# Attention weights turned by a transposing transfer of 16-bit halves, and the last batch's query tiles taken one by one

## The chip, the core and the metric

The kernel runs on one core of a Trainium2 chip. The metric is device time in microseconds from launch to end. The core has TensorE (PE; its weight loads are listed apart as PEld), VectorE (DVE), ScalarE (ACT), GpSimd (POOL) and SyncE (SP), which here only issues transfers (DMAs). Each engine works through its own queue in order; engines wait for each other and for transfers through semaphores.

## What is computed

Top-k attention for 8 batches, 8 heads, 576 rows and head dimension 64, followed by a feed-forward layer on the 4608 x 512 result:

```python
scores = scale * np.matmul(q, k.transpose(0, 1, 3, 2))
kth = np.partition(scores, -top_k, axis=-1)[..., -top_k:-top_k + 1]      # top_k = 32
scores = np.where(scores >= kth, scores, -1000000000.0)
attn = np.exp(scores - np.max(scores, axis=-1, keepdims=True))
attn = attn / (np.sum(attn, axis=-1, keepdims=True) + 1e-09)
x = np.matmul(attn, v)                       # then (B,H,S,D) -> (B*S, H*D)
h = x @ w_in                                 # 512 -> 2048
g = np.where(h > 0.0, h, np.exp(np.minimum(h, 0.0)) - 1.0)
return (g @ w_out).astype(np.float32)        # 2048 -> 512
```

All of it is in 32-bit floats; the two weight matrices come in as 64-bit numbers and are converted at the start.

## The kernel before

**Steps.** The 576 rows of a batch make four query tiles of 128 rows and a rest of 64 (`rem`; the rests of an even batch and the next odd one fill one tile together). One step handles a query tile for two heads (a head pair, `hp`), or the rest for four heads: 128 partitions by two rows of 576 scores, the tile `u.sc`. A batch has 4 x 4 + 2 = 18 steps, the run 144 (`NS`). `orders` says in which order a batch takes its tiles: one by one, `(0,)`, or in pairs, `(0, 1)`, whose steps alternate within a head pair so that one attention product serves both (a `Group`).

**The loop** (lines 809 to 848) runs over n and works on four steps at once, in a pipeline written out by hand:

- step n + 2: `scores`, TensorE (L335) into one pair of PSUM tiles, then ScalarE copies to `u.sc` (L343). Five `sc` buffers.
- step n: `select`, VectorE, in four passes: eight searches for the eight largest (L355, L369) and six replacements (L362). Between the passes the loop issues everything else.
- step n - 1: `spread` (GpSimd L376), `mask` for each of the two rows (ScalarE L396 and L397, with the row's sum), `normalise` (GpSimd L407 to L414).
- step n - 2 (`done`): `turn`, which transposes the weights for the product with v. Nine blocks of 128x128 go through TensorE (L433) into PSUM, and ScalarE copies them to the group's `et` tile (L434), in three calls: four blocks (`main`) and one (`rest`) after the second pass, four (`other`) after the third. Two `et` buffers.
- `attend`, two iterations after a group was turned: TensorE multiplies `et` with `vT` (L459), ScalarE copies into the block's `xT` (L486).

**Feed-forward blocks.** Finished tiles are collected in blocks of one or two tiles (`division`), in the order of `ends`. A block's work comes as pieces: 16 hidden units (`hidden`, L534, then ScalarE L544, L547, L549, L553 and GpSimd L504), and for two tiles seven products by Strassen's scheme (`product`, L624; half of their weights come back from memory in tiles `tw`, prefetched six deep by `stream`, L666), for one tile four projections (`project`, L562). `feed`, called four times in an iteration, is the planner: each block has a due time `ready` in steps (3.25 after its last tile's last step), each piece a cost (`HIDDEN`, `PROJECT`), and `feed` issues as many pieces as keep the due times. What is left after the loop is issued at its end (line 849). Before, there are 21 blocks: five of one tile, fifteen of two, one of one.

**Keys and queries** of the coming batch are loaded a few iterations ahead (L235), and VectorE transposes them in 32x32 blocks (L289) into one of five `kqT` buffers; the previous user of a buffer is an older `scores`.

**Transfers** are all issued from SP's queue, in the order of the program: loads, `tw` prefetches, outputs.

**Start.** `tight` is 2 * NHP = 8 and `settled` 12; the first iterations do some of this in another order while the weights are converted. `settle` opens the pools that take the place of the raw weights.

Of the kernel before, what the change touches and what calls it, by code (L numbers as in the profile page):

```python
# [9 lines left out]
ALU = mybir.AluOpType  # L10
FP32 = mybir.dt.float32
U32 = mybir.dt.uint32
I32 = mybir.dt.int32
PSUM = bass.MemoryType.PSUM

# [65 lines left out]
def kernel(  # L81
# [41 lines left out]
    xpool = pool("x", 2)  # L123
    opool = pool("o", 2)
    scratch = pool("scratch", 1, space=bass.MemoryType.DRAM)
    ps_sc = pool("ps_sc", 1, space=PSUM)
    ps_t = pool("ps_t", 2, space=PSUM)
    ps_f = pool("ps_f", 2, space=PSUM)
# [89 lines left out]
    def decode_piece(i):  # L218
# [153 lines left out]

    def spread(u):

        u.den = small.tile([P, 4], FP32, tag="den", name="den")
        nc.gpsimd.tensor_tensor(  # L376
            u.den[:, 2:4], u.last[:, :, 7], u.first[:, :, 0], ALU.subtract
        )

    def mask(u, i, early=False):  # L380

        if u.masked:
            return
        if i == 0 and early:
            u.den = small.tile([P, 4], FP32, tag="den", name="den")  # L390
# [5 lines left out]
        nc.scalar.activation(sc, sc, AF.Prelu, scale=-1.0, bias=low, alpha=1.0 / STEEP)  # L396
        nc.scalar.activation(  # L397
            sc, sc, AF.Exp, scale=-STEEP, bias=gap, accum_out=u.den[:, i : i + 1]
        )

    def normalise(u):

        if u.normal:
            return
        u.normal = True
        den = small.tile([P, 2], FP32, tag="dene", name="dene")
        nc.gpsimd.tensor_scalar_add(den[:], u.den[:, 0:2], EPS)  # L407
        rec = small.tile([P, 2], FP32, tag="rec", name="rec")
        nc.gpsimd.tensor_tensor(rec[:], den[:], power[:], ALU.pow)
        nc.gpsimd.tensor_tensor(den[:], den[:], rec[:], ALU.mult)  # L410
        nc.gpsimd.tensor_scalar(den[:], den[:], -1.0, 2.0, ALU.mult, ALU.add)
        nc.gpsimd.tensor_tensor(rec[:], rec[:], den[:], ALU.mult)
        for i in range(2):
            nc.gpsimd.tensor_scalar(  # L414
                u.sc[:, i, :], u.sc[:, i, :], rec[:, i : i + 1], 1.0, ALU.mult, ALU.mult
            )

    def turn(u, chunks):

        if u.turned:  # L420
            return
        g = u.group
        if g.et is None:
            g.et = etpool.tile([P, 2 * J + 1, len(g.tiles), P], FP32, tag="et", name="et")
        if chunks.stop - chunks.start == 1:
            ps = wide[1][:, 1, HS : HS + P]
        else:
            ps = ps_t.tile([P, JP], FP32, tag="t", name="eps")
        sc = u.sc[:, :, :].rearrange("p i s -> p (i s)")
        n = chunks.stop - chunks.start  # L430
        for c in range(n):
            c0 = (chunks.start + c) * P
            nc.tensor.transpose(ps[:, c * P : (c + 1) * P], sc[:, c0 : c0 + P], ident[:])  # L433
        nc.scalar.copy(  # L434
            g.et[:, chunks, u.at, :],
            ps[:, 0 : n * P].rearrange("p (c q) -> p c q", c=n),
        )
        if chunks.stop == 2 * J + 1:
            u.turned = True
            if u.at == len(g.tiles) - 1:  # L440
                closing.append((place[0] // 4, g))

    def attend(g):
        t = g.tiles[0]
# [65 lines left out]
    def ffn_pieces(blk):  # L510
# [4 lines left out]
        def hidden(f):  # L515
# [32 lines left out]
            if end % unit == 0:  # L548
                nc.scalar.activation(blk.n, blk.n, AF.Exp, scale=-1.0)  # L549
                dst = g[:, end - unit : end, 0:n_tok]  # L550
                apart = place[0] > 4 * (tight + 3) and blk is not blocks[-1]
                if apart:
                    nc.scalar.activation(blk.n, blk.n, AF.Copy, bias=-1.0)  # L553
                gates.append((place[0], (blk.number, f + 1 - unit), dst, blk.n, apart))
# [254 lines left out]
    for n in range(NS + 3):  # L809
# [30 lines left out]
        next(passes)  # L840
        if prev:
            normalise(prev)
# [42 lines left out]
```

## Time and profile before

| | |
|---|---|
| runs, median of 3 (lowest, highest) | 1583.68 us (1582.25, 1584.01) |
| profiled execution, span from first to last instruction | 1583.3 us |
| instructions | 28148 |
| transfers on SP's queue | 121.38 MB |
| L433 (transposes on TensorE), busy | 175.7 us in 1152, 40.3 us in 144 |
| L434 (their copies on ScalarE), busy | 163.9 us in 288, 38.5 us in 144 |

In the profile, times are in us from the first instruction, unless marked ns. A row of a group gives line, engine, operation, output <- input with shapes and the count, then the busy time and the mean ns of one, then the idle time of the engine just before and what ended it. Rows of a stretch give, after its length, the busy time and count of TensorE, its weight loads, VectorE, ScalarE and GpSimd, then TensorE's granted clock, the transfer engines' busy share and GB/s. Rows of a timeline give start, length, engine, line, operation and count, and idle time with what ended it in brackets; a matmul's length contains its way through the array, so neighbours overlap, and the distance from start to start is what one costs. Waits are given as total us, number, longest.

### The profile page before, as it was taken

The page shows a single profiled execution, that of the slowest core. Times are in us where ns is not written, and L with a number is a line of the kernel's source. Part 1 is how long each engine was busy: PE and PEld are TensorE (multiplying, and loading weights), DVE is VectorE, ACT ScalarE, POOL GpSimd, SP SyncE. Part 2 cuts the span into 40 slices and gives each one's busy share as a digit, 9 for nine tenths or more (in the row PEclk, how much of TensorE's full clock was granted, in tenths as well). Part 3 has the DMA queues.
Part 4 walks back from the last instruction along what each step waited for, and adds up shares of the span by engine and source line. Part 5 has one row for each costly group of instructions (what it writes and reads, how often), then busy time and mean ns, then how long its engine had stood idle before and what let it go on. Part 6 is the DMA issues. An engine that isn't in the chain of part 4 may idle for free.

```text
span 1583.3 us, 28148 instructions
## 1 busy us (share of the span) xinstructions
PE 1522.8 (96%) x9492; PEld 1189.1 (75%) x9492; DVE 1450.6 (92%) x2976; ACT 1189.6 (75%) x2460; POOL 901.2 (57%) x1551
## 2 busy tenths in 40 slices
PE   4789989999999999999999999999999999999999
PEld 2477667767777778877887788877777777887786
DVE  6899999999999999999999799999999789999600
ACT  6897678768696968696878787868777777878642
POOL 4983455555656565656565647564646555656550
PEclk9879999999999999999999999999999999999999
DMA  8622202231504141334223412314140514030311
GB/s 244 191 81 37 38 28 57 55 88 39 154 4 136 31 124 28 96 69 110 57 81 71 108 50 79 96 54 105 34 125 9 142 27 132 9 120 1 120 53 34
DMA packets 224910, 123.46 MB, mean 78 GB/s; under 512 B 182272, under 2 KB 183296, under 8 KB 224768
## 3 DMA queue, kind: packets, MB, share of 16 engines
q1 hardware_dynamic: 223568, 121.38, 28.6%
q8 instruction: 75, 1.23, 0.3%
q14 instruction: 67, 0.55, 0.1%
q10 hardware_dynamic: 1200, 0.30, 0.1%
HBM read 108.00 MB, written 13.63 MB: 77 GB/s over the span
## 4 chain that ended last, share of the span: by engine, by line
PE 71%; DVE 17%; ACT 5%; issue 3%; POOL 3%; DMA 0%; SPq 0%; DVEq 0%; POOLq 0%; ACTq 0%
PE hps L534 25%; PE ops L624 23%; PE avps L459 9%; PE scps L335 9%; DVE wk L362 8%; DVE m L369 6%; PE eps L433 5%; DVE m L355 2%; ACT sc L397 1%; POOL sc L414 1%; DVE raw L192 1%; PE scps L433 1%; ACT et L434 1%; POOL gT L504 1%; ACT sc L396 0%
## 5 line engine op out<-in xcount | busy, mean ns | idle before, releaser
L369 DVE MAX8 m<-wk 128x8 f32<-128x576 f32 x864 | 609.6, 747 | 0.0
L534 PE MATMUL hps<-xT,w_in 128*128 128x256 f32 (+1 forms) x2688 | 550.0, 354 | 0.0
L534 PEld LDWEIGHTS hps<-xT,w_in 128*128 128x128 f32 x2688 | 444.3, 192 | 64.1 <-issue 22.7
L362 DVE MATCH_REPLACE8 wk<-m,wk 128x576 f32<-128x576 f32 x576 | 423.5, 743 | 0.0
L407 POOL TENSOR_SCALAR dene<-den 128x2 f32<-128x2 f32 x144 | 32.3, 225 | 411.4 <-ACT sc L397 410.2
L397 ACT ACTIVATE sc<-sc,den 128x576 f32<-128x576 f32 x288 | 223.5, 776 | 52.6 <-POOL den L376 40.0
L335 PE MATMUL scps<-kqT 64*128 64x288 f32 (+1 forms) x1280 | 211.5, 447 | 37.4 <-ACT et L434 23.3
L396 ACT ACTIVATE sc<-sc,m 128x576 f32<-128x576 f32 x288 | 224.9, 781 | 28.7 <-DVE m L369 28.7
L414 POOL TENSOR_SCALAR sc<-sc,rec 128x576 f32<-128x576 f32 x288 | 213.5, 751 | 14.9
L624 PE MATMUL ops<-tw,gT 128*128 128x256 f32 x960 | 219.8, 382 | 1.9 <-issue 1.9
L355 DVE MAX8 m<-sc 128x8 f32<-128x576 f32 x288 | 202.0, 743 | 11.8 <-ACT sc L343 11.8
L362 DVE MATCH_REPLACE8 wk<-m,sc 128x576 f32<-128x576 f32 x288 | 211.6, 743 | 0.0
L624 PEld LDWEIGHTS ops<-tw,gT 128*128 128x128 f32 x960 | 177.8, 190 | 32.6 <-issue 6.5
L343 ACT ACTIVATE sc<-scps 128x576 f32<-128x576 f32 x288 | 170.8, 646 | 37.4 <-PE scps L335 37.3
L459 PE MATMUL avps<-et,vT 128*64 128x256 f32 (+2 forms) x2320 | 191.9, 314 | 2.9 <-ACT et L434 2.9
L504 POOL TENSOR_TENSOR gT<-n,gT 128x512 f32<-128x512 f32 x136 | 173.5, 1276 | 35.9 <-ACT n L553 35.9
L335 PEld LDWEIGHTS scps<-kqT 64*128 64x128 f32 (+1 forms) x1280 | 112.5, 183 | 105.1 <-ACT et L434 33.5
L459 PEld LDWEIGHTS avps<-et,vT 128*64 128x64 f32 x2320 | 130.0, 142 | 72.8 <-issue 36.0
L433 PE MATMUL eps<-ident,sc 128*128 128x128 f32 x1152 | 175.7, 277 | 2.1 <-POOL sc L414 1.6
L433 PEld LDWEIGHTS eps<-ident,sc 128*128 128x128 f32 x1152 | 143.4, 143 | 34.2 <-issue 7.0
L434 ACT COPY et<-eps 128x512 f32<-128x512 f32 x288 | 163.9, 569 | 6.3 <-PE eps L433 5.8
L624 PE MATMUL ops<-w_out,gT 128*128 128x256 f32 x720 | 165.4, 383 | 0.0
(56 smaller groups left out, 1534.3 us busy)
## 6 DMA issues: line engine op xcount, KB each, us to landing
tw<-kept SPq DMA_DIRECT2D x240, 256.0 KB, 3.0
raw<-in_moe_w_in_dram SPq DMA_DIRECT2D x16, 512.0 KB, 4.9
vT<-in_v_dram SPq DMA_DIRECT2D x64, 128.0 KB, 2.5
raw<-in_moe_w_out_dram SPq DMA_DIRECT2D x16, 512.0 KB, 4.4
out_dram<-osb SPq DMA_DIRECT2D x32, 256.0 KB, 3.7
kin<-in_k_dram SPq DMA_DIRECT2D x112, 72.0 KB, 2.8
qin<-in_q_dram SPq DMA_DIRECT2D x112, 72.0 KB, 2.6
kept<-tw SPq DMA_DIRECT2D x16, 256.0 KB, 2.1
```

The source lines that it names most:

```text
L335: nc.tensor.matmul(wide[i][rows, half, 0:HS], kq[part, q0 : q0 + u.t.ql], kq[part, k0 : k0 + HS], start=True, stop=True,)
L355: nc.vector.max(found[i], cur[i])
L362: nc.vector.match_replace(wk[i], found[i], cur[i], TAKEN)
L369: nc.vector.max(found[i], cur[i])
L396: nc.scalar.activation(sc, sc, AF.Prelu, scale=-1.0, bias=low, alpha=1.0 / STEEP)
L397: nc.scalar.activation(sc, sc, AF.Exp, scale=-STEEP, bias=gap, accum_out=u.den[:, i : i + 1])
L414: nc.gpsimd.tensor_scalar(u.sc[:, i, :], u.sc[:, i, :], rec[:, i : i + 1], 1.0, ALU.mult, ALU.mult)
L433: nc.tensor.transpose(ps[:, c * P : (c + 1) * P], sc[:, c0 : c0 + P], ident[:])
L459: nc.tensor.matmul(ps[i * D : (i + 1) * D, cols], vt[:, 2 * J + i if c == J else i * J + c, :], w, start=(c == 0), stop=(c == J),)
L504: nc.gpsimd.tensor_tensor(dst, n, dst, ALU.add)
L534: nc.tensor.matmul(blk.h[:, f % bank, :], w_in[:, i, f * P : (f + 1) * P], blk.xT[:, i, 0:n_tok], start=(i == 0), stop=(i == NC - 1),)
L624: nc.tensor.matmul(sums, x[:, f, :], w, start=opens and f == 0, stop=f == NG - 1, skip_group_check=not opens,)
```

## The change

1. *Turning.* In iterations n > `settled`, `turn` is replaced. `split(done, 0)`, before the first pass, and `split(done, 1)`, after the second, each copy one row's 576 words on ScalarE into a tile of two planes of 16-bit halves (`planes`, one buffer, low halves then high halves) and write it from SP to a tile in device memory (`halves`, three buffers). `cross(done)`, after the third pass, reads that tile back with one transposing transfer of 16-bit elements, 256 rows (query, half) by 1152 columns (row of scores, key), into the group's `et` tile: 9 blocks of 128 partitions by 256 halves, which are 128 words. Nothing of the weights' value is changed.
2. *Last batch.* Its query tiles are taken one by one, as the first batch's are, and the last five tiles make five blocks of one tile. There are then 23 blocks: five of one tile, thirteen of two, five of one.
3. *Small things.* The denominator's helper columns live in one tile of eight columns; the condition under which a block's gates are closed on GpSimd is now `blk.ready < NS` instead of `blk is not blocks[-1]`.

```diff
+    halves = pool("halves", 3, space=bass.MemoryType.DRAM)
...
+        late["p"] = ctx.enter_context(tc.tile_pool(name="p", bufs=1))
...
-        den = small.tile([P, 2], FP32, tag="dene", name="dene")
-        nc.gpsimd.tensor_scalar_add(den[:], u.den[:, 0:2], EPS)
-        rec = small.tile([P, 2], FP32, tag="rec", name="rec")
+        den, rec = u.den[:, 4:6], u.den[:, 6:8]
+        nc.gpsimd.tensor_scalar_add(den, u.den[:, 0:2], EPS)
...
+    def split(u, i):
+
+        if u.turned:
+            return
+        if i == 0:
+            u.halves = halves.tile([P, 2, 2, S], U16, tag="h", name="halves")
+        t = late["p"].tile([P, 2, S], U16, tag="p", name="planes")
+        words = u.sc[:, i, :].bitcast(U16).rearrange("p (k w) -> p w k", w=2)
+        nc.scalar.copy(t[:], words)
+        nc.sync.dma_start(u.halves[:, :, i, :], t[:])
+
+    def cross(u):
+
+        if u.turned:
+            return
+        g = u.group
+        if g.et is None:
+            g.et = etpool.tile([P, 2 * J + 1, len(g.tiles), P], FP32, tag="et", name="et")
+        nc.sync.dma_start_transpose(
+            g.et[:, :, u.at, :].bitcast(U16),
+            u.halves[:].rearrange("q w i k -> (q w) (i k)"),
+        )
+        turned(u)
+
+    def turned(u):
+
+        u.turned = True
+        if u.at == len(u.group.tiles) - 1:
+            closing.append((place[0] // 4, u.group))
...
-                apart = place[0] > 4 * (tight + 3) and blk is not blocks[-1]
+                apart = place[0] > 4 * (tight + 3) and blk.ready < NS
...
-        if b == 0:
+        if b in (0, B - 1):
             order = [(0,), (1,), (2,), (3,)]
...
-        n = 1 if len(blocks) <= J else 2
+        n = 1 if len(blocks) <= J or len(ends) <= J + 1 else 2
...
+        crossed = n > settled
+        if done and crossed:
+            split(done, 0)
         next(passes)
         feed(n, 0.25)
...
-        if done:
+        if done and not crossed:
             turn(done, main)
             turn(done, rest)
+        elif done:
+            split(done, 1)
         if prev:
             mask(prev, 1, n <= tight)
         next(passes)
         feed(n, 0.25)
-        if done:
+        if done and not crossed:
             turn(done, other)
+        elif done:
+            cross(done)
```

More of the change, by code (lines that the diff above doesn't have):

```diff
@@ L12 @@
 U32 = mybir.dt.uint32
+U16 = mybir.dt.uint16
 I32 = mybir.dt.int32
@@ L373, in spread @@
     def spread(u):
-        u.den = small.tile([P, 4], FP32, tag="den", name="den")
+        u.den = small.tile([P, 8], FP32, tag="den", name="den")
         nc.gpsimd.tensor_tensor(
@@ L389, in mask @@
         if i == 0 and early:
-            u.den = small.tile([P, 4], FP32, tag="den", name="den")
+            u.den = small.tile([P, 8], FP32, tag="den", name="den")
         u.masked = i == 1
@@ L405, in normalise @@
         u.normal = True
-        den = small.tile([P, 2], FP32, tag="dene", name="dene")
-        nc.gpsimd.tensor_scalar_add(den[:], u.den[:, 0:2], EPS)
-        rec = small.tile([P, 2], FP32, tag="rec", name="rec")
[L409 to L412, printed above, removed]
+        den, rec = u.den[:, 4:6], u.den[:, 6:8]
+        nc.gpsimd.tensor_scalar_add(den, u.den[:, 0:2], EPS)
+        nc.gpsimd.tensor_tensor(rec, den, power[:], ALU.pow)
+        nc.gpsimd.tensor_tensor(den, den, rec, ALU.mult)
+        nc.gpsimd.tensor_scalar(den, den, -1.0, 2.0, ALU.mult, ALU.add)
+        nc.gpsimd.tensor_tensor(rec, rec, den, ALU.mult)
         for i in range(2):
@@ L438, in turn @@
         if chunks.stop == 2 * J + 1:
-            u.turned = True
-            if u.at == len(g.tiles) - 1:
-                closing.append((place[0] // 4, g))
+            turned(u)
[18 more added lines that the diff above has]
+        )
+        turned(u)
+    def turned(u):
+        u.turned = True
+        if u.at == len(u.group.tiles) - 1:
+            closing.append((place[0] // 4, u.group))
     def attend(g):
```

## The prediction

> **What bounds the kernel now.** I read the busy table, then the busy times by stretch, then who waited for whom, and last the order of time around the end.
>
> ```profile
> PE 1522.8 (96%) x9492; PEld 1189.1 (75%) x9492; DVE 1450.6 (92%) x2976; ACT 1189.6 (75%) x2460; POOL 901.2 (57%) x1551
> ```
> ```profile
> 0.00:80.00 80.00, 46.45 (x193) 30.53 (x194) 63.13 (x126) 61.05 (x123) 53.36 (x84) 0.91 0.71 215
> 80.00:800.00 720.00, 706.62 (x4563) 542.91 (x4563) 720.00 (x1479) 563.20 (x1164) 413.46 (x738) 0.98 0.27 68
> 800.00:1300.00 500.00, 493.17 (x2998) 391.70 (x2997) 475.33 (x977) 383.68 (x796) 289.89 (x500) 1.00 0.30 77
> 1300.00:1480.00 180.00, 177.34 (x1176) 143.25 (x1175) 180.00 (x374) 139.10 (x291) 110.02 (x189) 1.00 0.24 72
> 1480.00:1584.00 104.00, 99.19 (x568) 80.67 (x568) 12.13 (x24) 42.53 (x88) 34.43 (x44) 1.00 0.19 59
> ```
> ```profile
> DVE kqT L289 <- PE scps L335: 24.7, 2, 16.6
> ```
> ```profile
> 1487.95 1.41 DVE L369 MAX8 m<-wk 128x8 f32<-128x576 f32 x2
> ```
> ```profile
> 1484.69 3.62 PE L624 MATMUL ops<-tw,gT 128*128 128x256 f32 x16
> 1488.24 2.38 PE L459 MATMUL avps<-et,vT 128*64 128x256 f32 x20
> ...
> 1519.43 1.31 PE L459 MATMUL avps<-et,vT 128*64 128x128 f32 x20
> 1520.67 3.72 PE L534 MATMUL hps<-xT,w_in 128*128 128x256 f32 x16
> ...
> 1551.57 14.45 PE L534 MATMUL hps<-xT,w_in 128*128 128x128 f32 x128
> 1565.87 13.90 PE L562 MATMUL ops<-w_out,gT 128*128 128x512 f32 x32
> ```
> ```profile
> 1579.85 0.58 ACT L571 COPY osb<-ops 128x512 f32<-128x512 f32 x1 [12.18 <-issue]
> 1580.46 0.33 SPq L574 DMA_DIRECT2D out_dram<-osb  x1
> ```
>
> Two engines are full at once. VectorE's top-k search ends at 1489.4 us (1487.95 + 1.41), and up to there it stood still for only 41.5 us: 16.9 in the first 80 us (80 − 63.13), and 24.7 between 800 and 1300, where the key and query transposes of L289 waited for TensorE's scores. TensorE is the one that is late: when VectorE has finished, TensorE is only at the attention product of 1488.24, where iteration 143 begins, so it lags by one iteration, and has 91.5 us of work left (to 1579.8). Copy and store add 3.5 us to the span of 1583.3. So the span is 1447.8 us of VectorE work before the search ends (1450.6 less 2.8 of gates in the tail), 41.5 of stalls, and a tail of 93.9.
>
> **The change, part by part.** *Turning, from iteration 13 on.* The condition is `n > settled`, with `settled` = 8 + 4, so the steps 11 to 143 change, 133 of 144. (The change's few words say 21; I count by the code.) Off TensorE go nine transposes a step, off ScalarE three copies:
>
> ```profile
> 700.35 0.60 PE L433 MATMUL eps<-ident,sc 128*128 128x128 f32 x4
> 700.79 0.27 PE L433 MATMUL scps<-ident,sc 128*128 128x128 f32 x1
> 700.90 1.89 PE L534 MATMUL hps<-xT,w_in 128*128 128x256 f32 x8
> 702.63 0.60 PE L433 MATMUL eps<-ident,sc 128*128 128x128 f32 x4
> 703.06 1.89 PE L534 MATMUL hps<-xT,w_in 128*128 128x256 f32 x8
> ```
> ```profile
> 702.88 0.57 ACT L434 COPY et<-eps 128x512 f32<-128x512 f32 x1
> 703.34 0.27 ACT L434 COPY et<-scps 128x128 f32<-128x128 f32 x1
> 703.50 0.78 ACT L396 ACTIVATE sc<-sc,m 128x576 f32<-128x576 f32 x1
> ...
> 705.09 0.57 ACT L544 ACTIVATE n<-hps 128x512 f32<-128x512 f32 x1
> ...
> 707.24 0.57 ACT L434 COPY et<-eps 128x512 f32<-128x512 f32 x1
> 707.70 1.19 ACT L343 ACTIVATE sc<-scps 128x576 f32<-128x576 f32 x2
> ```
>
> Start to start, since neighbours overlap, that is 0.44 + 0.11 + 0.43 = 0.98 us of TensorE and 0.62 + 0.46 = 1.08 us of ScalarE a step: 130 and 144 us in all.
>
> ScalarE gets two copies of 1152 half-words (`split`), a form that the trace lacks:
>
> ```profile
> L396 ACT ACTIVATE sc<-sc,m 128x576 f32<-128x576 f32 x288 | 224.9, 781 | 28.7 <-DVE m L369 28.7
> L553 ACT ACTIVATE n<-n 128x512 f32<-128x512 f32 x136 | 85.8, 631 | 4.3
> L184 ACT ACTIVATE w_in<-raw 128x512 int32<-128x512 uint32 x16 | 10.6, 663 | 0.0
> ```
>
> The two L434 copies give 0.30 us for 384 more elements (0.46 less 0.16), 0.78 ns each, so 1152 from L553's 0.63 come to 1.13 us, and 1.04 start to start. That is the low end; the high end is L396 twice over, 1.56. L184 reads every second word and costs 5% more than L553, so I stay near the low end: 1.04. ScalarE then has 1189.6 − 144 + 277 = 1323 us, below VectorE's need. Behind a `split` on ScalarE's queue stand the next mask and the FFN's activations, and for those TensorE's banks wait. The first copy of a step waits for GpSimd's normalising of the iteration before:
>
> ```profile
> 1495.44 0.23 POOL L407 TENSOR_SCALAR dene<-den 128x2 f32<-128x2 f32 x1 [5.85 <-ACT sc L397]
> ...
> 1497.39 1.48 POOL L414 TENSOR_SCALAR sc<-sc,rec 128x576 f32<-128x576 f32 x2
> ```
>
> Its first half is ready 2.7 us after the mask (1495.44 to 1497.39, and half of 1.48); the score copies and FFN activations in between cover that. The second waits until the first write has left the one `planes` buffer; a mask (1.6 us), two feeds and mostly the wait for VectorE lie between. In an iteration with two groups of FFN hidden units ScalarE has two masks of 1.6 (703.50 to 705.09), two `split`s, score copies of 1.2 and two groups of 2.15 (705.09 to 707.24), 10.8 us against VectorE's 10.1 (1447.8 / 144), so over the four such iterations of a block it falls back some 3 us, and recovers in the products. The scores are two iterations ahead and absorb this, except where L289 needs the newest scores; for that I add 3 us.
>
> SP's queue gets three transfers a step:
>
> ```profile
> q1 hardware_dynamic: 223568, 121.38, 28.6%
> ```
> ```profile
> DMA packets 224910, 123.46 MB, mean 78 GB/s; under 512 B 182272, under 2 KB 183296, under 8 KB 224768
> ```
> ```profile
> tw<-kept SPq DMA_DIRECT2D x240, 256.0 KB, 3.0
> kin<-in_k_dram SPq DMA_DIRECT2D x112, 72.0 KB, 2.8
> kept<-tw SPq DMA_DIRECT2D x16, 256.0 KB, 2.1
> ```
>
> Two writes of 288 KB in runs of 1152 B land like `kept<-tw`, in 2.1 to 2.4 us. The transposing transfer of 576 KB is unknown. Its bounds: q1's mean rate, 121.38 MB in 28.6% of the span or 268 GB/s, gives 2.2 us of all sixteen engines; cut into 128-byte packets (72 KB key loads consist of these), 4608 at q1's mean of 32 ns give 9.3 us. Its source rows lie in one piece of 2304 B, nearest to the 2 KB rows of `tw`, so I take 2.2, landing in about 4. A step of 10.1 us has 7.2 us free of the present 28.6%, and the writes take 2.2, so 5 are left. In front of the reader lies more than an iteration: `cross` comes in the third quarter of n, `attend` at n + 2.
>
> `cross` makes SP wait for the second write, 2 to 3 us, and behind it on SP stand the `tw` prefetches (six tiles ahead, 0.9 us of TensorE each), key and query loads (four iterations early), value loads and outputs. A prefetch that is late by 3 us sometimes stops TensorE; it has the room shown below. If that room were gone, it is the third rival.
>
> *The last batch.* Query tiles one by one and five blocks of one tile replace two blocks of two (tiles 7,4 with 7,0 and 7,1 with 7,2). A single block takes 28.2 us (1551.57 to 1579.8). A block of two takes 16 hidden units of 1.73 (700.90 to 702.63) and seven products of 3.55 (1484.69 to 1488.24), 52.5. So two times 3.9 more, and four attention products of 1.25 twice instead of 2.31 once, 0.8: TensorE pays 8.6 us. What counts is what may start only at the end: before, a block of two and a single one; now two singles.
>
> *No time:* the denominator's columns in one tile (the same five GpSimd operations), and `blk.ready < NS` (only the last block, at 147.25, is out, as before).
>
> **The sum.** TensorE: 1522.8 − 130 + 8.6 = 1401 us. Of that 60 come after the search, so 1341 plus 33.6 idle in the first 80 us must fit before it: 90 us or 0.7 a step to spare. Then the 24.7 us of L289 vanish, and the search ends at 1489.4 − 24.7 + 3 = 1467.7. By the planner's own due times, worked through for the new blocks, TensorE has at the start of iteration 144 still 14 hidden units of 0.90 and the four projections (13.9) of the block of tile 7,2, four attention products of 1.25, and the last block, 28.2: 59.7 us. The last weights need, after the search, two masks and a `split` between (4.5), GpSimd (2.7 to the first half), `split`, write, `split`, write (6.8) and the transfer (4 to 5): 18 to 19 us, and TensorE gets to them after 20. With 3.5 for copy and store the tail is 63.2. The sum is 1467.7 + 63.2 = **1531 us**, 52 below the span of this execution, which is the runs' median within 0.4 us.
>
> **Rivals.** *The transposing transfer is slow.* Were it cut as fine as the key loads, 9.3 us, a step would need 2.9 + 2.2 + 9.3 = 14.4 us of the transfer engines against 10.1: 133 × 4.3 = 570 us more, some 2100 us. It decides from about 5.4 us on, where 133 steps lose the 52 us. For it: no transfer of this kind is in the trace. Against: long source rows, rings three quarters idle. The Trainium skill, "VectorE: DVE Perf Modes", The three transpose paths, gives 1309 ns for one 128x128 of 16 bits by transfer, against 390 on TensorE; 18 such one after another would be an estimated 23.6 us a step, and some 3300 us in all. "DMA: Bandwidth & Descriptors", Latency and other measured facts, gives 261 GB/s for whole transposing transfers, about q1's rate here. No run so far shows which holds.
>
> *ScalarE becomes the bound.* With 1.56 us a copy it has 1189.6 − 144 + 415 = 1461 us, all of the time to the end of the search, and it also waits in order; at 97% use the search ends near 1506 and the time is about 1570. For it: 75% busy, growing most where it is fullest. Against: L184 and L553.
>
> *SP holds up TensorE.* Thirteen blocks of two with two late prefetches of 3 to 4 us each give 80 to 100 us, the whole room; the stalls of L289 return and the time is near 1560 to 1585.
>
> *Only the tail is won*, because L289 still waits for other reasons: 1531 + 22 = 1553.
>
> **How the numbers follow.** Forecast 0.60 (own range 1516 to 1548: TensorE one iteration ahead or behind its place at the end, 9 us, and a late last transfer). Only the tail 0.08. ScalarE 0.10 (0.07 faster, 0.01 same, 0.02 slower). SP 0.07 (0.04, 0.02, 0.01). Slow transfer 0.15, all slower. About 0.2% is what a measurement of this kernel tells from no change. Faster 0.79, same 0.03, slower 0.18. The range runs from 1516 to 1592: it leaves out the slow transfer and some 0.05 beside it.
>
> **What would show it.** Right: TensorE's L433 rows are left with 11 steps, its busy time is near 1400; the `split` rows read near 1.1 us; the transposing transfer's median to landing is under 6 us; L289 waits for nothing; VectorE's search ends near 1468 and TensorE's tail is two blocks of 28 us. Wrong: VectorE waiting for score copies over many steps with the transfer share near 1 (slow transfer), ScalarE over 97% busy, or SP's waits passed on to L624.

## The result and the profile after

| | before | after |
|---|---|---|
| median (lowest, highest) | 1582.97 us (1582.16, 1584.01), 4 runs | 1837.77 us (1836.1, 1838.11), 4 runs |
| span of the profiled execution | 1583.3 us | 1835.6 us |
| predicted | | 1531 (1516 to 1592) |

The ratio is 1.1608, with a 95% interval of 1.1592 to 1.1624. The kernel became 255 us slower where 52 us less were forecast.

The busy table of the kernel after, engine by engine:

```profile
PE 1496.8 (82%) x8535; PEld 1109.2 (60%) x8535; DVE 1460.6 (80%) x2976; ACT 1316.5 (72%) x2321; POOL 875.2 (48%) x1535
```

No engine is full any more. VectorE has the same work as before (1460.6 against 1450.6) and now stands still for a fifth of the span. The stretch in the middle of the run, with the columns of the view of before:

```profile
200.00:1700.00 1500.00, 1218.51 (x6852) 914.86 (x6853) 1234.87 (x2526) 1086.99 (x1885) 718.89 (x1272) 0.92 0.61 156
```

There VectorE works 82% of the time, TensorE 81%, ScalarE 72%, the transfer engines 61%: a loop of waits, not a full engine. The view of waits names them (us in total, times, longest):

```profile
ACT planes L451 <- DMA halves<-planes: 245.1, 93, 8.0
DVE m L358 <- ACT sc L346: 221.0, 79, 11.9
...
PE ops L654 <- DMA tw<-kept: 79.2, 20, 10.8
...
DVE kqT L292 <- PE scps L338: 51.7, 3, 24.3
...
PE avps L489 <- DMA et<-halves: 48.9, 29, 4.0
```

The reader follows it backwards. VectorE waits for ScalarE's copies of the scores (221.0) and at the key transposes for TensorE's scores (51.7); ScalarE waits 245.1 us at its half-word copies, nearly all of it at the second one of a step, for the write of the first, because there is one `planes` buffer; and TensorE has a wait that it did not have before, for the prefetched tiles `tw`. The two VectorE waits together, 272.7 us, are nearly the whole of the 276.5 us by which the search ends later than forecast: at 1742.76 + 1.41 = 1744.2 instead of 1467.7 (11.8 us of them stand at the start of the kernel before too).

```profile
1742.76 1.41 DVE L372 MAX8 m<-wk 128x8 f32<-128x576 f32 x2
```

What the queues do shows in the waits of SP, first of the kernel before, then of the one after:

```profile
SPq L666 <- PE ops L624: 686.5, 222, 52.5
```
```profile
SPq L452 <- ACT planes L451: 452.4, 157, 6.8
SPq L461 <- DMA halves<-planes: 242.2, 110, 5.4
...
SPq L696 <- PE ops L654: 18.8, 33, 1.3
```

Before, SP stood at the next `tw` prefetch and waited for TensorE to free a tile: whenever TensorE took one, the next load left at once. After, SP stands at ScalarE's copies and at the writes, and reaches the prefetch when the tile has long been free (18.8 us of waiting in place of 686.5). With each `tw` load paired in the trace with the product that freed its tile, the load left 0.03 us (median) after that before the change, and 5.1 us after it; 143 of the 208 were over 3 us late. At TensorE's 20 waits for `tw` the loads were 7.2 us late on average and took 3.1 us to land, where the median before was 3.0: what stops TensorE is the late issue and not a slow transfer. The new issues in the view of one tile (nanoseconds least/median/most of SP's own time, then first and last start, then a column that is empty here):

```profile
L452 SPq DMA_DIRECT2D halves<-planes x266: 533/553/1033, 171.6 to 1785.1; - x133
L461 SPq DMA_TRANSPOSE et<-halves x133: 2115/2536/4354, 178.2 to 1787.7; - x133
```

133 steps between 171.6 and 1785.1 are some 12.2 us a step (the last two lie behind the end of the search), against 10.1 forecast. One step in the order of time (start, length, engine; the idle time and what ended it in brackets):

```profile
845.31 5.42 PE L654 MATMUL ops<-tw,gT 128*128 128x256 f32 x24
...
847.99 1.15 ACT L451 COPY planes<-sc 128x1152 uint16<-128x1152 uint16 x1 [1.43 <-POOL sc L416]
848.59 2.15 SPq L238 DMA_DIRECT2D kin<-in_k_dram  x4
...
850.84 2.07 SPq L238 DMA_DIRECT2D qin<-in_q_dram  x4
...
853.01 0.55 SPq L452 DMA_DIRECT2D halves<-planes  x1
...
853.66 2.03 SPq L696 DMA_DIRECT2D tw<-kept  x4
...
855.76 1.15 ACT L451 COPY planes<-sc 128x1152 uint16<-128x1152 uint16 x1 [4.72 <-DMA halves<-planes]
...
856.60 3.78 PE L654 MATMUL ops<-tw,gT 128*128 128x256 f32 x8 [5.87 <-DMA tw<-kept]
...
860.31 1.32 PE L338 MATMUL scps<-kqT 64*128 64x288 f32 x8
...
862.35 1.42 DVE L358 MAX8 m<-sc 128x8 f32<-128x576 f32 x2 [3.58 <-ACT sc L346]
```

The first copy is done at 849.14, but its write leaves only at 853.01: SP is issuing eight key and query loads, which the program places ahead of it. So ScalarE stands 4.72 us before the second copy; the `tw` loads, which come behind the write in the program, leave at 853.66, three microseconds after TensorE has used up its tiles (845.31 + 5.42 = 850.7), and TensorE stands 5.87 us; the next scores come behind that product, at 860.31, and VectorE waits 3.58 us for them. Summed over the trace's rows, the first write of a step starts 1.8 us after its copy's end on average, 238 us in all: 124 us of it directly behind query loads (26 times), 75 behind value loads (22) and 22 behind a transposing transfer (19). ScalarE's other work covers some 3.1 us between the two copies: where the first write left within 0.3 us (55 steps), the second copies waited 22 us in all; where it left over 3 us late (40 steps), 177.

### The profile page after: what moved, and what is told of

It reads as the page before. It is cut to its first block, busy times and chain, and to the rows that moved or that the text cites. A ratio compares the mean times of both kernels' runs of the same rounds, so it can differ in the third digit from the quotient of the medians.

```text
span 1835.6 us, 26765 instructions
## 1 busy us (share of the span) xinstructions
PE 1496.8 (82%) x8535; PEld 1109.2 (60%) x8535; DVE 1460.6 (80%) x2976; ACT 1316.5 (72%) x2321; POOL 875.2 (48%) x1535
## 4 chain that ended last, share of the span: by engine, by line
ACT 26%; PE 22%; DMA 18%; DVE 11%; POOL 10%; SPq 7%; issue 6%; DVEq 0%; ACTq 0%; POOLq 0%
DMA halves<-planes 14%; ACT planes L451 8%; PE ops L654 8%; PE hps L564 5%; DVE wk L365 5%; ACT sc L399 4%; ACT sc L400 4%; PE ops L592 4%; DVE m L372 3%; PE avps L489 3%; DMA tw<-kept 3%; POOL sc L416 2%; SPq L238 2%; PE scps L338 2%; ACT sc L346 2%
## 5 line engine op out<-in xcount | busy, mean ns | idle before, releaser
L564 PE MATMUL hps<-xT,w_in 128*128 128x256 f32 (+1 forms) x2944 | 574.1, 354 | 96.1 <-ACT gT L577 91.7
L564 PEld LDWEIGHTS hps<-xT,w_in 128*128 128x128 f32 x2944 | 487.6, 203 | 179.2 <-ACT gT L577 104.0
L451 ACT COPY planes<-sc 128x1152 uint16<-128x1152 uint16 x266 | 306.8, 1153 | 308.7 <-DMA halves<-planes 245.1
L358 DVE MAX8 m<-sc 128x8 f32<-128x576 f32 x288 | 203.3, 747 | 222.4 <-ACT sc L346 221.0
L410 POOL TENSOR_SCALAR den<-den 128x2 f32<-128x2 f32 x144 | 32.3, 225 | 719.6 <-ACT sc L400 718.5
L654 PEld LDWEIGHTS ops<-tw,gT 128*128 128x128 f32 x832 | 167.1, 207 | 141.2 <-DMA tw<-kept 89.1
L489 PE MATMUL avps<-et,vT 128*64 128x128 f32 (+2 forms) x2400 | 199.3, 316 | 53.5 <-DMA et<-halves 48.9
L416 POOL TENSOR_SCALAR sc<-sc,den 128x576 f32<-128x576 f32 x288 | 213.5, 751 | 14.9
L489 PEld LDWEIGHTS avps<-et,vT 128*64 128x64 f32 x2400 | 138.8, 145 | 124.6 <-issue 52.9
L654 PEld LDWEIGHTS ops<-w_out,gT 128*128 128x128 f32 x624 | 125.5, 207 | 78.8 <-POOL den L410 26.7
L592 PE MATMUL ops<-w_out,gT 128*128 128x512 f32 x320 | 145.1, 606 | 0.7 <-POOL tw L711 0.7
```

The costliest lines, as they stand in the source:

```text
L416: nc.gpsimd.tensor_scalar(u.sc[:, i, :], u.sc[:, i, :], rec[:, i : i + 1], 1.0, ALU.mult, ALU.mult)
L451: nc.scalar.copy(t[:], words)
L489: nc.tensor.matmul(ps[i * D : (i + 1) * D, cols], vt[:, 2 * J + i if c == J else i * J + c, :], w, start=(c == 0), stop=(c == J),)
L564: nc.tensor.matmul(blk.h[:, f % bank, :], w_in[:, i, f * P : (f + 1) * P], blk.xT[:, i, 0:n_tok], start=(i == 0), stop=(i == NC - 1),)
L592: nc.tensor.matmul(blk.o[:], blk.gT[f // NG][:, f % NG, s * P : (s + 1) * P], w_out[:, f, :], start=(f == 0), stop=(f == NF - 1),)
L654: nc.tensor.matmul(sums, x[:, f, :], w, start=opens and f == 0, stop=f == NG - 1, skip_group_check=not opens,)
```

## The experiments

Every kernel below differs from the one after, or from an earlier experiment where that is said, by the diff shown; the diffs give the lines that matter, with `...` where some between them are left out. A time without a number of runs beside it is a single run; runs of the kernel before, taken beside them, lie between 1582 and 1586 us.

**Which of the two parts loses.** `e1_last_only` keeps only the last batch's order and single blocks; `e2_turn_only` keeps only the turning.

```diff
-        crossed = n > settled
+        crossed = False
```
```diff
-        if b in (0, B - 1):
+        if b == 0:
...
-        n = 1 if len(blocks) <= J or len(ends) <= J + 1 else 2
+        n = 1 if len(blocks) <= J else 2
```

> The last batch one by one and five last blocks of one tile, every step turned on TensorE as before. If the loss lies wholly in the new way of turning, this is not slower than before: TensorE pays 8.6 us more, the tail falls from 93.9 to about 70, so 1560 to 1575. If the single blocks are themselves a loss (TensorE was full), 1585 or more.

> The transposing transfer alone, last batch as before. If the loss lies wholly in the turning, 1837 plus the 10 to 25 us that the last batch's order wins: 1845 to 1865, with ScalarE waiting some 245 us for the planes buffer as in the changed kernel. If the two parts hurt each other, below 1800.

e1: 1587.3 us (1586.29 to 1587.65, 10 runs), ratio 1.0023 (1.0013 to 1.0032). e2: 1854.4. The loss is wholly in the turning; the last batch's part is worth 17 us beside it, and by itself costs 3. The last search of e1 says why:

```profile
1497.56 1.41 DVE L372 MAX8 m<-wk 128x8 f32<-128x576 f32 x2
```

TensorE is as full as before, with 3 us more work (1526.0 against 1522.8), and the shorter tail (1585.4 less 1499.0, 86.4 us against 93.9) is paid by a search that ends 9.6 us later (1499.0 against 1489.4).

**The loads ahead of the first write.** `e3_loads_after` issues the iteration's loads behind the first copy and write.

```diff
     for n in range(NS + 3):
-        for fn, args in todo.pop(n, []):
-            fn(*args)
...
             split(done, 0)
+        for fn, args in todo.pop(n, []):
+            fn(*args)
```

> Only the order on SP's queue is changed: an iteration's key, query and value loads are issued behind the first write of the planes, not ahead of it. Theory of the order: in the changed kernel the first write starts on average 1.8 us after its copy has ended, 238 us in all, nearly all of it behind these loads; ScalarE's wait for the planes falls from 245 us to 100 to 150, and the time to 1700 to 1760. Rival, ScalarE's work is too much: the time stays above 1810. Rival, the transfer engines are too full (their share 0.63): writes still take 2.8 us and more, the time stays above 1810.

1735.0 us, 103 less. The waits:

```profile
DVE m L358 <- ACT sc L346: 124.1, 50, 11.8
ACT planes L451 <- DMA halves<-planes: 121.9, 78, 5.4
...
PE ops L654 <- DMA tw<-kept: 74.3, 23, 10.5
```

ScalarE's wait for the first write is halved and VectorE's falls by 97, nearly the whole gain; the wait for `tw` stays. First writes still leave 81 us late in all, 58 of it directly behind the transposing transfer of the step before.

**The second copy later.** `e4_split_late` puts the second copy behind the second mask, in the third quarter, and the transposing transfer at the end of the iteration.

```diff
-        elif done:
-            split(done, 1)
         if prev:
             mask(prev, 1, n <= tight)
...
         elif done:
-            cross(done)
+            split(done, 1)
...
         feed(n, 0.25)
+        if done and crossed and late_cross:
+            cross(done)
```

> The second copy of a step comes a quarter later, behind the second mask, and the transposing transfer at the end of the iteration; loads still ahead of the first write. Theory of the one planes buffer: between the two copies there are now two masks, 3.3 us, and FFN work, more than the 2.7 us of a write that starts in time, so ScalarE's wait for the planes falls to 60 to 120 us (what the loads hold up beyond 5 us stays) and the time to 1650 to 1720. Rival, SP is held up by the wait in front of the transposing transfer and its 2.7 us of issue: prefetches of tw are as late as before, the time stays above 1780.

1862.6 us, slower, against my expectation.

```profile
ACT planes L451 <- DMA halves<-planes: 304.5, 160, 7.1
```

The wait grew from 245.1 to 304.5 and from 93 times to 160: with two writes an iteration through one buffer, a copy moved away from one write stands before the next. Here the next step's first copies wait 130 us for the second write, and the second copies still 175 for the first. Moving the copy does not cure it. The run moves the transposing transfer too, and TensorE's wait for `et` grows from 48.9 to 151.1 us; the two moves were not timed apart here.

**No wait for the buffer.** When the second copy begins, row 0 of the score tile is dead. `e5_dead_row` writes the second planes there; `e6_dead_loads` adds e3's order.

```diff
-        t = late["p"].tile([P, 2, S], U16, tag="p", name="planes")
+        if i == 0:
+            t = late["p"].tile([P, 2, S], U16, tag="p", name="planes")[:]
+        else:
+            t = u.sc[:, 0, :].bitcast(U16).rearrange("p (w k) -> p w k", w=2)
```

> The second copy of a step writes its planes over the first row of the score tile, which is dead by then, so that no copy waits for the write of the other; loads are ahead of the first write as in the changed kernel. Theory of the one buffer: ScalarE's wait for planes falls from 245 us to under 40, the time to 1640 to 1720. Rival, the moved loads are the cause and the buffer only passes their delay on: as the write is still late, the transposing transfer and the attention product are late instead, the time stays above 1760.

> Dead row, and the loads behind the first write. Theory of the one buffer: without it the order of the loads matters little, so within 25 us of the kernel with the dead row alone. Rival, order and buffer add: 60 us or more below it. In both, TensorE's wait for tw of some 75 us stays, since the wait ahead of the transposing transfer stays on SP.

1711.4 and 1717.6 us. With the wait for `planes` gone, the order of the loads is worth nothing (6 us the wrong way): the 103 us of e3 and the 126 of e5 are largely the same loss, met at two places. But the wait has moved, and VectorE still waits behind it, here in e5:

```profile
ACT sc L346 <- DMA halves<-sc: 121.4, 60, 6.7
...
DVE m L358 <- ACT sc L346: 95.3, 47, 11.7
```

The score tile is now held until the second write has read it.

**The transposing transfer later.** `e7_cross_late` is e3 with `cross` at the iteration's end (as in e4); `e8_all_three` is e6 with it.

> One planes buffer, loads behind the first write (1735 us so far), and the transposing transfer issued at the end of the iteration, behind the last quarter's prefetches. If SP's wait for the second write (245 us) makes prefetches late, TensorE's wait for tw falls from 74 us to under 40 and the time to 1690 to 1715. If ScalarE's chain sets the pace, the time stays within 15 us of 1735, and the attention products wait more for et.

> Dead row, loads behind the first write, transposing transfer at the end of the iteration. If these three waits are the whole of the loss, the sum of the prediction holds again: 1531 to 1570. If something else is left (ScalarE's work in order, transfer engines), 1600 or more.

1780.0 (45 more than e3) and 1726.5 (9 more than e6), both outside what was expected of a cure. In e7 TensorE waits 102.8 us for `et`, in e3 67.0:

```profile
PE avps L488 <- DMA et<-halves: 102.8, 33, 8.3
...
PE ops L653 <- DMA tw<-kept: 66.6, 18, 9.4
```

The wait for `tw` only falls from 74.3 to 66.6 (second row): moving `cross` does not free the `tw` loads, and later it is itself too late.

**Another queue for the prefetch.** `e9_tw_act` is e3 with the `tw` loads issued from ScalarE.

```diff
-        nc.sync.dma_start(t[:], src[:].rearrange("p (f n) -> p f n", f=TF))
+        nc.scalar.dma_start(t[:], src[:].rearrange("p (f n) -> p f n", f=TF))
```

> Loads behind the first write (1735 us), and the prefetches of tw issued from ScalarE's queue in place of SP's. Theory of the shared queue: SP now stands at ScalarE's copies and at the transposing transfer, so a prefetch that TensorE has made room for is issued up to an iteration late; from another queue TensorE's wait for tw falls from 74 us to under 20, and the time to 1650 to 1690. Rival, the transfers themselves are slow beside the new traffic (tw lands in 3.8 us against 3.0): the wait stays above 50 us and the time above 1715.

1779.1 us, slower than e3 by 44.

```profile
ACT planes L451 <- DMA halves<-planes: 175.8, 75, 6.3
...
PE ops L654 <- DMA tw<-kept: 41.8, 19, 6.9
```

TensorE's wait fell by 32, but ScalarE, which now also issues, waits 54 us more. ScalarE is where SP stood: a load still leaves 4.1 us (median) after its tile is free, as in e3, so that changing the queue leaves the prefetch tied to the same place in the program.

**A second planes buffer, and its control.** `e10_planes2` is e3 with two `planes` buffers; the room comes from five `tw` tiles instead of six and a smaller pool. `e18_control` has the same room taken away, but one `planes` buffer.

```diff
-    TF, TB = 2, 6
+    TF, TB = 2, 5
...
-        late["p"] = ctx.enter_context(tc.tile_pool(name="p", bufs=1))
+        late["p"] = ctx.enter_context(tc.tile_pool(name="p", bufs=2))
```

> Loads behind the first write, and two planes buffers (paid for by five tw tiles in place of six and fewer small buffers). Neither copy waits for the other's write, nor does a score tile wait for one. If the one buffer is the main loss: ScalarE's wait for planes under 15 us, time 1620 to 1680. If SP's queue is the main loss, the wait goes and the time stays above 1690, with TensorE's wait for tw at 75 us or more.

> Loads behind the first write, one planes buffer, and the five tw tiles and fewer small buffers of the kernel with two. If these two are harmless, 1725 to 1745 (1735 without them), and the second buffer is worth some 40 us; if five tiles make prefetches later, 1760 or more, and the second buffer is worth that much more.

1693.3 and 1750.2 us: the second buffer is worth 57, the room taken from the prefetch and the small pool costs 15 (e18 against e3). ScalarE's wait for the write is down to 3.3 us in e10; TensorE's for the prefetch is no smaller, as the second of the two cases expected:

```profile
PE ops L655 <- DMA tw<-kept: 81.0, 22, 10.8
...
DVE m L359 <- POOL den L380: 62.1, 35, 4.4
...
DVE kqT L293 <- PE scps L339: 48.3, 3, 20.4
```

VectorE hardly waits for score copies any more (16.6 us), but for GpSimd to read the results of earlier steps, of which the smaller pool holds fewer, and at the key transposes as in the kernel after.

**More queues.** `e11_tw_act_planes2` is e10 with e9's edit; `e12_and_loads_pool` moves the key and query loads to GpSimd as well (`nc.gpsimd.dma_start` at L238).

> Both: two planes buffers and the prefetches on ScalarE's queue. If buffer and queue are the two causes: 1550 to 1610, TensorE's wait for tw under 20 us. If ScalarE's own work sets the pace by now (1316 us and the issues of the prefetches), 1620 to 1660, with ScalarE over 85% busy and no wait of its own above 50 us.

> As the last one, and key and query loads issued from GpSimd's queue: SP has only writes, transposing transfers, values and outputs. If SP's 4.4 us of issue for a head pair's loads still delays writes: 10 to 40 us below the last one. If GpSimd's normalising is held up by the issues instead: not faster, with ScalarE's wait for L416 above 60 us.

1698.5 and 1698.1 us: no gain, and e11 lies above both of its forecasts. In e11 TensorE's wait moved from `tw` (81.0 to 31.4 us) to `et` (66.9 to 99.3):

```profile
PE avps L490 <- DMA et<-halves: 99.3, 31, 8.9
```

In e12 ScalarE's wait for GpSimd's L417 grew from 46.7 to 85.7 us, the second of its two cases.

**How much is the prefetch?** `e13_no_prefetch` is e10 without the `tw` loads after the first five: the products read those five tiles again, so a part of the weights in them is not the right one.

```diff
-                        t = streamed.pop(0)
+                        t = streamed[taken[0]]
+                        taken[0] += 1
...
+        if k >= TB:
+            streamed.append(streamed[-TB])
+            return
```

> Two planes buffers, loads behind the first write (1693 us), and the prefetches of tw left out after the first five: the products read the same five tiles over and over, so that part of the weights is wrong. Theory of the tied prefetch: TensorE's 81 us of waiting for tw go and with them ScalarE's and GpSimd's waits for products; 1600 to 1640. Rival, ScalarE's work sets the pace: above 1665.

1578.8 us, 114 less than e10, less than either case allowed, and level with before. Its busy table and VectorE's waits:

```profile
PE 1414.1 (90%) x8535; PEld 1063.5 (67%) x8535; DVE 1451.9 (92%) x2976; ACT 1307.6 (83%) x2321; POOL 878.9 (56%) x1535
```
```profile
DVE kqT L293 <- PE scps L339: 12.5, 2, 12.2
...
DVE m L359 <- POOL den L380: 9.0, 8, 2.3
```

Of e10's two waits of VectorE, 110.4 us, 21.5 are left: they hung on the prefetch. The run removes the tiles' lateness, their issue and their bytes together, and does not say which of the three it is. That e11 made the loads less late (1.7 us at the median, e10 3.3) without a gain speaks against lateness alone.

**How much is ScalarE's work?** `e14_half_copy` is e10 with half of each row copied; the planes are two fixed tiles, zeroed once, so that the second half of the keys is zero in them and left out of the attention product. `e16_pool_split` is e10 with the copies on GpSimd.

```diff
-        nc.scalar.copy(t[:], words)
+        nc.scalar.copy(t[:, :, 0:HS], words[:, :, 0:HS])
```
```diff
-        nc.scalar.copy(t[:], words)
+        nc.gpsimd.tensor_copy(t[:], words)
```

> Two planes buffers, loads behind the first write, and only the first half of each plane copied (576 of 1152 elements), the other half left at zero; all transfers as before. It takes 0.48 us from each of 266 copies, 128 us of ScalarE. Theory of ScalarE's work: the time falls by 80 us or more, to 1610 or less. Theory of the tied prefetch: by 0 to 40 us, to 1650 to 1693.

> Two planes buffers, loads behind the first write, the copies to planes made by GpSimd, behind its own normalising. ScalarE has 1010 us of work left. Theory of ScalarE's work: 1600 to 1640, unless GpSimd's copies take over 2 us each (then GpSimd is the bound, its busy time above 1400). Theory of the tied prefetch: 1670 or more, since SP then stands at GpSimd's copies.

1645.1 (48 less than e10) and 1661.8 (31 less), both between the two theories. Less work on ScalarE helps, but TensorE's wait for `tw` stays (74.8 and 96.2 us, e10 81.0).

**Fewer steps.** `e15_every_third` is e3 with every third step turned by transfer. `e17_hidden_only` is e16 with a step turned by transfer only where the next piece of feed-forward work is a hidden unit, which reads no `tw`; where it is a product or a projection, where none is in the queue, and in the last two steps, TensorE turns as before.

```diff
-        crossed = n > settled
+        crossed = n > settled and n % 3 == 0
```
```diff
-        crossed = n > settled
+        crossed = settled < n < NS and bool(ffn) and ffn[0][0] < PROJECT / 1.5
```

> One planes buffer, loads behind the first write, only the steps of every third iteration turned by transfer, the others on TensorE. TensorE is relieved of 43 us, ScalarE gets 54 more. If the waits only cost where slack is used up, 1550 to 1580, faster than before. If each turned step costs its share (152 us over 133 steps, 1.1 us each), 1583 plus 50, some 1630.

> Copies on GpSimd, two planes buffers, loads behind the first write, and the transposing transfer only in iterations where the feed-forward piece at the head of the queue is a hidden unit; where products come, and at the end, TensorE turns as before. If the tied prefetch is what is left, TensorE's wait for tw falls below 25 us and the time to 1555 to 1590. If every turned step costs about 1.1 us for other reasons as well, 1610 to 1640.

e15: 1631.4 us (1627.1 to 1635.5, 4 runs), ratio 1.0292 (1.0266 to 1.0318). Against e1, 1587.3, its 44 turned steps cost 1.0 us each. e17: **1557.66 us** (1556.96 to 1564.39, 4 runs), ratio 0.9848 (0.9825 to 0.9872): 1.5% below the kernel before, and clear of the noise. It turns 69 of the 133 steps by transfer. From e1 to e17 the time falls by 29.6 us, 0.43 for each of these 69, with the other changes of e16 (order of the loads, buffers, copies on GpSimd) in it; from e17 to e16 the other 64, beside products or projections or with nothing in the queue, lose 104 us, 1.6 each. That points to what TensorE reads while the transfers are issued, and not to their number alone; a run of e16 with 69 steps spread evenly, which would tell the two apart, was not made. The busy table of e17, TensorE's wait for `tw`, SP's first wait and the stretch from 800 to 1300:

```profile
PE 1459.4 (94%) x9111; PEld 1116.0 (72%) x9111; DVE 1451.5 (93%) x2976; ACT 1114.0 (72%) x2247; POOL 1030.4 (66%) x1673
```
```profile
PE ops L655 <- DMA tw<-kept: 7.8, 3, 6.8
```
```profile
SPq L697 <- PE ops L655: 238.5, 180, 11.6
```
```profile
800.00:1300.00 500.00, 485.32 (x2904) 383.04 (x2903) 498.49 (x1027) 371.01 (x755) 357.15 (x574) 1.00 0.54 140
```

TensorE's wait for `tw` is below the 25 us expected. SP again waits ahead of TensorE at the prefetch (180 times; 184 in e1, which has the same blocks), a load leaves 0.03 us (median) after its tile is free, as before the change, and VectorE is full, 498.5 of 500.

## Why the prediction was wrong, step by step

- **The size of the new work was about right.** ScalarE's copy was taken at 1.04 us and is 1.15 (row below). That its total came out at 1316.5 against 1323 is partly luck: 307 us were added where 277 were forecast, and L434's copies, booked by their distance and not their length, took 187 away and not 144. TensorE was forecast at 1401 us: it has 1414.1 in e13, but 1496.8 in the kernel after, for the same 8535 matmuls at a lower granted clock (0.919, e13 0.968). The writes land in 2.6 us, taken at 2.1 to 2.4. The view of groups, then of the issues with their median to landing, of the kernel after:

```profile
L451 ACT COPY planes<-sc 128x1152 uint16<-128x1152 uint16 x266 | 306.8, 1153 | 308.7 <-DMA halves<-planes 245.1
```
```profile
halves<-planes SPq DMA_DIRECT2D x266, 288.0 KB, 2.6
...
et<-halves SPq DMA_TRANSPOSE x133, 4.7
```

- **The rival of a slow transposing transfer fell.** It lands in 4.7 us, taken at "about 4". The Trainium skill, "VectorE: DVE Perf Modes", The three transpose paths, would have 18 blocks of 1309 ns, an estimated 23.6 us; the trace does not agree when they go as one transfer. What my step left out is SP's own time for it, 2.5 us at the median, with which a step's three issues take 3.6 us (2.5 and twice 0.55) of the queue. The transfer engines' time was right for a wrong reason. I argued from long source rows, but in the trace each transposing transfer is 2304 packets of 256 bytes, some 2.95 us of all sixteen engines, and the two writes take 1.7: 4.7 a step against 4.4 forecast. My bound of 9.3 priced small packets at the queue's mean of 32 ns; the 128-byte packets of the kernel before took 12.7 each. The queue's line of the kernel after:

```profile
q1 hardware_dynamic: 602000, 269.92, 56.3%
```

- **The step that failed first** is "The second waits until the first write has left the one `planes` buffer; a mask (1.6 us), two feeds and mostly the wait for VectorE lie between", costed at nothing. The cover, some 3.1 us, just holds a write of 2.6 that leaves at once, but I counted it from the copy's end and not from the write's start. What the program puts ahead of the write on SP, loads above all, holds it up by 1.8 us a step, up to 8. I listed what stands *behind* the new transfers and never what stands *ahead* of the write. Price: 245 us of ScalarE's waiting, and 103 (e3) to 126 us (e5) of time, as far as these two runs remove it: half of the wait is left in e3, and in e5 it has moved to the score tile.
- **The second failure is the size of the prefetch rival,** "SP holds up TensorE", at 0.07 and 80 to 100 us of stalls. I priced it as two late prefetches a block of 3 to 4 us each. In fact the tie is lasting: SP now follows ScalarE's place in the program, and a `tw` load cannot leave before ScalarE has copied, however early TensorE has freed the tile. The quoted 686.5 us of SP waiting for TensorE was to be seen before, and was the room that the change used up. The prefetch's whole price, with the buffer's wait gone, is 114 us (e13); the tie's share of it was not measured. My line for a wrong outcome, "SP's waits passed on to L624", is what came, with the score copies as a second sign.
- **"90 us or 0.7 a step to spare"** was the room for all of this, and too small for the two together: on average, a step is 2.1 us longer than forecast. And the loop has only two steps of scores in hand, so ScalarE's and TensorE's delays reach VectorE. "In front of the reader lies more than an iteration" also failed: TensorE waits 48.9 us for `et` in the kernel after, and still 56.9 in e13.
- **The end of the search at 1467.7** is nearly reached in e17, at 1471.0: L289's wait is 1.5 us, though TensorE is freed there in 69 steps alone. No run shows it for the change as forecast, with all 133 steps turned: e13, without the prefetch, ends the search at 1487.6. The views of e17, the last search and the transposes' group:

```profile
1469.60 1.41 DVE L373 MAX8 m<-wk 128x8 f32<-128x576 f32 x2
```
```profile
L293 DVE STREAM_TRANSPOSE kqT<-kin 128x576 f32<-128x576 f32 x28 | 21.3, 761 | 1.5 <-PE scps L339 1.5
```

- **The tail of 63.2 us was mis-sized.** It is 1835.6 − 1744.2 = 91.4 after, and 84.4 in e17 (1555.4 − 1471.0). TensorE's rows of the kernel after from the end of the search:

```profile
1745.01 7.03 PE L592 MATMUL ops<-w_out,gT 128*128 128x512 f32 x16
...
1753.21 7.13 PE L592 MATMUL ops<-w_out,gT 128*128 128x512 f32 x16
...
1769.21 2.40 PE L489 MATMUL avps<-et,vT 128*64 128x128 f32 x20 [4.05 <-DMA et<-halves]
...
1803.85 14.45 PE L564 MATMUL hps<-xT,w_in 128*128 128x128 f32 x128
1818.14 13.90 PE L592 MATMUL ops<-w_out,gT 128*128 128x512 f32 x32
```

  The four projections of the block before (14.2 us) are still ahead of the two blocks of 28 that I counted, and TensorE waits there for `et` and gates, 7.0 us. I had the planner one set of projections further on than it was. In e1 it shows alone: the tail falls by 7.5 us and not by 30, and the search ends later.
- **The denominator's columns and the gates' condition** were costed at nothing; e1, which contains both, is 3 us slower than before in all. They were not tried apart.

The account from the kernel after to before: 1837.8, 103 for the order of the loads (1735.0), 42 for a second buffer with its room taken from the prefetch (1693.3), 114 for the prefetch (1578.8). The order of the subtractions matters: e5 shows that the first two overlap. Of the 48 us that e13 still lies above the forecast, 20 are the search's end (1487.6) and 26 the tail. The first are VectorE's two waits in e13 shown above, 21.5 us where 3 were allowed for. What delays TensorE and GpSimd there was not settled; ScalarE's work may be part of it, since e14 and e16, with less of it, were 48 and 31 us faster than e10. It also stays open how the 114 us divide between late tiles, SP's time and the transfer engines.

## What to carry to other kernels

A transfer that waits for an engine, put on a queue that issues in order, ties everything behind it to that engine's place in the program: before adding one, read for whom the queue waits now, since a prefetch whose issuer waits long for its reader loses just that lead. Count a write's lateness from what stands ahead of it on its queue, and with one buffer between copy and write take that lateness as the copying engine's. If the tie cannot be removed, use the new path only where the tied work isn't read: here that step took the time from 1661.8 (e16) to 1557.7 us, 1.5% below the kernel before, while it also halved the number of such transfers.

## What the runs showed of the hardware

- A transposing transfer of 256 rows by 1152 16-bit columns (576 KB, device memory to on-chip tile) lands in 4.7 us at the median. The Trainium skill, "DMA: Bandwidth & Descriptors", Latency and other measured facts, has 261 GB/s for a transposing transfer with a non-contiguous middle dimension and 350 to 400 for a contiguous one, an estimated 2.3 us and 1.5 to 1.7 us here. The trace does not agree: the packets alone, 2304 of 256 bytes, take some 2.95 us of the sixteen engines, about 200 GB/s. Of the 4.7 us, 2.5 are SP's issue.
- GpSimd copies 1152 strided half-words about as fast as ScalarE, 1145 against 1153 ns. The group of e16:

```profile
L452 POOL COPY planes<-sc 128x1152 uint16<-128x1152 uint16 x266 | 303.2, 1145 | 17.6 <-DMA halves<-planes 17.6
```

- Where TensorE waits often, its granted clock is lower: 0.92 between 200 and 1700 us, where before it had 0.98 to 1.00. The matmuls with `tw` take 419 ns at the mean instead of 382. Their median is 379 in both; of the 832 after, 155 took over 450 ns, up to 796 (before, 29 of 960), and 126 of these began within 4 us of the end of a wait of over 1 us (126 of the 254 that began there, 29 of the other 578). A wait here is thus followed by slower matmuls, as in the step above, where the 8 behind the wait took 3.7 us; that the wait is the cause was not tried apart. The groups of before and after:

```profile
L624 PE MATMUL ops<-tw,gT 128*128 128x256 f32 x960 | 219.8, 382 | 1.9 <-issue 1.9
```
```profile
L654 PE MATMUL ops<-tw,gT 128*128 128x256 f32 x832 | 219.2, 419 | 97.1 <-DMA tw<-kept 79.2
```
